# Hash attention and a squared-ReLU MLP: the first pair of heads loaded six tokens to a partition, its successor's preparation and the weight sums placed elsewhere

## The chip, the core and the metric

The kernel runs on one core of a Trainium2 chip. A core has four compute engines that each work through their own instruction stream in order: TensorE (PE, with a separate row PEld for its weight loads), VectorE (DVE), ScalarE (ACT) and GpSimd (POOL). SyncE (SP) issues DMAs, and ACT and POOL issue some too. The metric is device time in microseconds. Before the change it is 879.85 us, the median of three runs (879.66 to 879.92).

## The reference

```python
batch, n_heads, seq, head_dim = (4, 8, 768, 64)       # q, k, v in float32, proj is 64 x 6
n_tokens, d_model, d_ff = (3072, 512, 2048)           # w_in, w_out

q_bits = (np.einsum('bhsd,dk->bhsk', q, proj) > 0)    # k_bits likewise
mask = q_bucket[:, :, :, None] == k_bucket[:, :, None, :]
scores = scale * np.matmul(q, k.transpose(0, 1, 3, 2))
scores = np.where(mask, scores, -1000000000.0)
attn = np.exp(scores - max); attn = attn / (sum + 1e-09)
attn_out = np.matmul(attn, v)
x = attn_out.transpose(0, 2, 1, 3).reshape(B * S, H * D)
h = x @ w_in;  r = np.maximum(h, 0.0);  out = (r * r) @ w_out
```

A query sees only the keys whose six sign bits equal its own. The order of the keys makes no difference to the result, as long as keys and values have the same order.

## The kernel before

**Two stages.** The attention stage (to about 331 us) goes over 16 pairs of heads, `for pr in range(NP)` at L614. The MLP stage after it multiplies by `w_in` and `w_out` with a Strassen-like scheme of seven products in place of eight; its weights' sums are made in the attention stage.

**One pair.** q and k have the two heads' 64 features on 128 partitions and 768 tokens along the row (`feat[pr, 0]` and `feat[pr, 1]`). `hash_bits` (L337) multiplies them by `proj`, `signs` (L351, eight ACT instructions for a pair) turns the products into bits, and `weigh` (L379) scales the keys' bits. For each of six key tiles `kt`, `score(pr, kt)` (L386) puts the product of the bits plus the product of the features into PSUM in two pieces (512 and 256 queries), and ACT takes the exponential of each into a ring of four tiles `e` (L413). `add_up` (L419) sums the tiles on DVE into `total`. `attend` (L432) multiplies by the values. `finish(pr)` (L579) runs one pair late: the column sums of `total` (`tot`, L455), their transpose `flip` and reciprocals on DVE, the last two `attend`s and `spread`. `normalize` (L483) writes `x_t`.

**PSUM.** `turn` (L104) hands out three buffers of two banks in rotation, for the score pieces, the hash products, the first pair's transposes and `tot`. An instruction that writes a buffer waits until the buffer's last reader is done.

**Preparation of the next pair.** From pair 1 on, `features(pr + 1, w)` (L330, a 32 x 32 block transpose on DVE) stands at the head of the round, and `prepare()` (L618: hash products and signs of the next pair) is issued inside `finish`. For pair 0 they stand elsewhere: the two `features(1, w)` before `add_up(0, 1)` (L641), and `prepare()` between `score(0, 2)` and `score(0, 3)` (L656).

**The first pair's start.** Its q and k come in with tokens on partitions: `load_first` (L267) issues q's two heads on the SP and the ACT queue, then k's two heads, then `proj`. Each descriptor is 256 bytes, one token of one head. `first_features` (L302) transposes three 128 x 128 blocks (both heads side by side) into PSUM; ACT copies q's (L316), DVE copies k's (L318). While the first load is on its way `keep_busy(8)` (L323) multiplies ones, and `keep_busy(2)` does so between q's and k's transposes. `first_keys` (L361) makes the keys' bits on DVE for this pair. The program's order on PE: eight busy products, six transposes of q, two busy products, three of k, the hash of q, the hash of k's first half, three transposes of k, the two feature products of key tile 0, its two bit products.

**The weights' sums.** Each pair rounds two pieces of the MLP weights on DVE (`round_weight`, `part_weight`; in the middle `place_power` on ACT). The dictionary `sums` (L542 to L547) says how many of the sixteen sums of the `w_in` factors (`sum_in`, L522: one 128 x 512 DVE operation and two DMAs on SP each) a pair makes: from pair 4 on one, two for pairs 6, 9 and 12, and the rest, two, for pair 15. They stand at the head of the round, ahead of `score(pr, 0)` and `finish(pr - 1)` in DVE's order.

Of the kernel before, what the change touches and what calls it, by code (L numbers as in the profile page):

```python
# [8 lines left out]
FP32 = mybir.dt.float32  # L9
# [25 lines left out]
def kernel(  # L35
# [10 lines left out]
    nc = tc.nc  # L46
    PSUM = bass.MemoryType.PSUM

    B, H, S, D = q.shape
# [3 lines left out]
    P = 128  # L53
    SB = S // P
    HS = S // 2
    NFT = DM // P
    NFF = DFF // P
    NP = B * H // 2
# [12 lines left out]
    ident = glob.tile([P, P], FP32, name="ident")  # L71
# [20 lines left out]
    p_qk = first.enter_context(tc.tile_pool(name="p_qk", bufs=2))  # L92
# [11 lines left out]
    def turn(name):  # L104

        return ps_s.tile([P, 2, 512], FP32, name=name, tag="turn")
# [4 lines left out]
    NIN = 2 * NFT  # L111
# [153 lines left out]
    nat, feat, bits = {}, {}, {}  # L265

    def load_first():  # L267

        for src, name in ((q, "q_nat"), (k, "k_nat")):
            t = p_qk.tile([P, SB, 2, D], FP32, name=name)  # L270
            for h, queue in enumerate((nc.sync, nc.scalar)):
                queue.dma_start(
                    out=t[:, :, h], in_=src[0, h].rearrange("(t p) d -> p t d", t=SB)
                )
            nat[0, name] = t
        for h, queue in enumerate((nc.sync, nc.scalar)):
            queue.dma_start(out=projs[h * D:(h + 1) * D, 0:NBITS], in_=proj)
# [15 lines left out]
    def load_values(pr):  # L293
        b, j = divmod(pr, PB)
        t = p_v.tile([P, 2, SB * D], FP32, name="v_nat")
        nc.sync.dma_start(
            out=t.rearrange("p h (t d) -> p (h t) d", d=D),
            in_=v[b, 2 * j:2 * j + 2].rearrange("h (t p) d -> p (h t) d", t=SB),
        )
        nat[pr, "v_nat"] = t  # L300

    def first_features(w, r):  # L302

        if r == 0:
            feat[0, w] = p_f.tile([P, S], FP32, name=f"feat{w}")
        tp = turn("tp")[:, 0]
        for i in range(SB // 2):
            t = r * (SB // 2) + i
            nc.tensor.transpose(  # L309
                out=tp[:, i * P:(i + 1) * P],  # L310
                in_=nat[0, ("q_nat", "k_nat")[w]][:, t].rearrange("p h d -> p (h d)"),
                identity=ident,
            )
        out = feat[0, w][:, r * HS:(r + 1) * HS]
        if w == 0:
            nc.scalar.copy(out=out, in_=tp[:, 0:HS])  # L316
        else:
            nc.vector.tensor_copy(out=out, in_=tp[:, 0:HS])  # L318

    busy = const.tile([P, 512], BF16, name="busy")  # L320
    void = ps_o.tile([P, 1024], FP32, name="xo")
# [8 lines left out]
    def features(pr, w):  # L330

        feat[pr, w] = p_f.tile([P, S], FP32, name=f"feat{w}")
        nc.vector.transpose(out=feat[pr, w], in_=nat[pr, ("q_nat", "k_nat")[w]])
# [52 lines left out]
    def score(pr, kt):  # L386

        e = ring[len(weights) % NRING]
        weights[pr, kt] = e
        key = slice(kt * P, (kt + 1) * P)  # L390
        sts = []

        def products(st, lo, hi, src, first):
            for h in range(2):
                rows = slice(h * D, (h + 1) * D)
                nc.tensor.matmul(  # L396
                    out=st[:, h, 0:hi - lo], lhsT=src[pr, 1][rows, key],
                    rhs=src[pr, 0][rows, lo:hi], start=first, stop=not first,
                )


        if (pr, kt) == (0, 0):
            for lo, hi in CUTS:
                sts.append(turn("st"))
                products(sts[-1], lo, hi, feat, True)
        for i, (lo, hi) in enumerate(CUTS):
            if len(sts) <= i:
                sts.append(turn("st"))
                products(sts[i], lo, hi, bits, True)
                products(sts[i], lo, hi, feat, False)  # L410
            else:
                products(sts[i], lo, hi, bits, False)
            nc.scalar.activation(  # L413
                out=e[:, :, lo:hi], in_=sts[i][:, :, 0:hi - lo], func=ACTF.Exp, scale=scale
            )
# [3 lines left out]
    def add_up(pr, kt):  # L419

        if kt == 1:
            totals[pr] = p_n.tile([P, 2, S], FP32, name="total")
            nc.vector.scalar_tensor_tensor(
                out=totals[pr], in0=weights[pr, 0][:, :, 0:S], scalar=SB * TINY,
                in1=weights[pr, 1][:, :, 0:S], op0=ALU.add, op1=ALU.add,
            )
        else:
            nc.vector.tensor_tensor(  # L428
                out=totals[pr], in0=totals[pr], in1=weights[pr, kt][:, :, 0:S], op=ALU.add
            )  # L430
# [17 lines left out]
    def sum_up(pr, tot):  # L448


        tot = tot[:, 0]
        for c in range(2):
            for h in range(2):
                g = 2 * h + c
                nc.tensor.matmul(  # L455
                    out=tot[g * 32:(g + 1) * 32, 0:HS], lhsT=ones,
                    rhs=totals[pr][:, h, c * HS:(c + 1) * HS], start=True, stop=True,
                )
        flip = p_n.tile([P, HS], FP32, name="flip")
        nc.vector.transpose(out=flip, in_=tot[:, 0:HS])  # L460
        once = p_n.tile([P, NB], FP32, name="once")
        nc.vector.reciprocal(
            out=once, in_=flip.rearrange("p (n f) -> p n f", f=32)[:, :, 0]
        )
        both = p_n.tile([P, 2, NB], FP32, name="both")
        nc.vector.tensor_tensor(
            out=both, in0=which,
            in1=once.rearrange("p (o n) -> p o n", o=1).to_broadcast([P, 2, NB]), op=ALU.mult,
        )
        onces[pr] = both  # L470
# [72 lines left out]
    todo = list(range(16))  # L543
    sums = {}
    for pr in range(NIN // 2, NP):
        n = 16 if pr == NP - 1 else 1 + (pr % 3 == 0)
        sums[pr], todo = todo[:n], todo[n:]  # L547

    xs = {}
# [22 lines left out]
    def sum_x(i, n):  # L572

        x, (t1, t2, t3) = xs[i]
        lo, hi = slice(0, NCH // 2), slice(NCH // 2, NCH)
        b11, b12, b21, b22 = x[:, 0:2, lo], x[:, 0:2, hi], x[:, 2:4, lo], x[:, 2:4, hi]
        minus(*((t1, b12, b11), (t2, b22, t1), (t3, b22, b12), (b12, b21, t2))[n - 1])

    def finish(pr, beside=None):  # L579

        tot = turn("tot")
        if beside:
            beside()
        sum_up(pr, tot)
        if pr == NP - 1:
            sum_x(0, 2)
            sum_x(0, 3)
        for kt in (SB - 2, SB - 1):
            attend(pr, kt)
        spread(pr)  # L590

    with tc.manual_schedule():
# [21 lines left out]
        for pr in range(NP):  # L614
            a, b = 2 * pr, 2 * pr + 1
            more = pr + 1 < NP

            def prepare():  # L618

                hash_bits(pr + 1, turn("hash"))  # L620
                for w in (1, 0):
                    signs(pr + 1, w)


            if pr + 2 < NP:
                load_pair(pr + 2)
            if pr == X_0:
                load_x(0)
            if more and pr > 0:
                for w in range(2):  # L630
                    features(pr + 1, w)
            if pr > 0:
                round_weight(b - 2)
                load_weight(b)
                for m in sums.get(pr, ()):
                    sum_in(m)
            score(pr, 0)
            if pr == 0:
                first_keys(1, turn("hash"))
            score(pr, 1)  # L640
            if pr == 0:  # L641
                for w in range(2):
                    features(1, w)
            if pr > 0:
                finish(pr - 1, prepare if more else None)
            add_up(pr, 1)
            if pr > 0:
                normalize(pr - 1)


            if pr == X_0 + 1:
                for n in range(2):
                    load_unit(n)
            part_weight(a)
            score(pr, 2)
            if pr == 0:  # L656
                prepare()
            score(pr, 3)
            if more and pr > 0:
                weigh(pr + 1)  # L660
            place_power(a)
            attend(pr, 0)
            attend(pr, 1)
            for kt in (2, 3):
                add_up(pr, kt)
            if more:
                load_values(pr + 1)


            round_weight(a)  # L670
            part_weight(b)
            if more:
                load_weight(a + 2)
            score(pr, 4)
            score(pr, 5)
            if pr == 0:
                weigh(1)
            place_power(b)
            attend(pr, 2)
            attend(pr, 3)  # L680
            add_up(pr, 4)
            add_up(pr, 5)
# [529 lines left out]
        for i in range(NCHUNK):  # L1212
            for s in range(NR):
                r = order(i * NR + s)
# [269 lines left out]
```

## Time and profile before

| what | value |
| --- | --- |
| median of the runs | 879.85 us |
| the profiled execution's own time | 879.66 us |
| its span in the trace | 877.9 us |
| PE busy | 864.8 us of the span |
| DVE busy | 760.4 us |
| ACT busy | 391.5 us |
| mean granted TensorE clock | 0.996 |
| first transposes of q on PE | 4.89 us |
| first exponential on ACT | 11.14 us |
| column sums of pairs 0, 1, 2 (`tot`) | 33.37, 53.28, 73.19 us |
| column sums of pairs 14, 15 | 311.26, 327.52 us |

The profile is of one execution. A row of the timeline has its start and its length in microseconds, the engine (with a q behind the name: the engine's sequencer, which waits or issues DMAs), the source line, the operation, the tiles it writes and reads, the shape, the number of merged instructions, and in brackets the idle time of the engine before it with what ended that. PE's records overlap, since matmuls are pipelined.

### The profile page before, as it was taken

How to read it: one execution, taken by the hardware profiler on the slowest of the kernel's cores; microseconds unless marked ns; L12 is line 12 of the kernel's file. 1: busy time of each engine (PE TensorE's matmuls, PEld its weight loads, DVE VectorE, ACT ScalarE, POOL GpSimd, SP SyncE). 2: the span in 40 equal slices, each digit the busy share in tenths (PEclk: the TensorE clock that was granted, in tenths of full speed). 3: DMA queues.
4: the chain of work that ended last, by engine and by line, in shares of the span. 5: the costliest groups of instructions: out<-in, count | busy, mean ns of one | idle time of the engine just before them, and what ended most of it. 6: DMA issues, size and time to landing. Idle time of an engine off the chain costs nothing.

```text
span 877.9 us, 12130 instructions
## 1 busy us (share of the span) xinstructions
PE 864.8 (99%) x4340; PEld 518.7 (59%) x4340; DVE 760.4 (87%) x1099; ACT 391.5 (45%) x673; POOL 107.0 (12%) x172
## 2 busy tenths in 40 slices
PE   8999999999999999999999999999999999999996
PEld 3444444444444444444688865556888755568885
DVE  5999999999999998888779968888889788888875
ACT  6988888888888852222211123332111233321110
POOL 2000000000000001554231011111000211110002
PEclk9999999999999999999999999999999999999998
DMA  9777967998788536999897764536756754355565
GB/s 176 142 149 134 233 153 156 188 253 225 179 176 225 156 105 213 299 267 283 292 353 239 181 160 168 173 118 222 285 151 187 167 165 155 124 167 154 158 175 105
DMA packets 224131, 167.09 MB, mean 190 GB/s; under 512 B 164448, under 2 KB 181344, under 8 KB 224064
## 3 DMA queue, kind: packets, MB, share of 16 engines
q1 hardware_dynamic: 189152, 87.19, 41.0%
q0 software_dynamic: 12528, 41.30, 15.2%
q10 hardware_dynamic: 22384, 37.76, 14.0%
q8 instruction: 36, 0.59, 0.3%
q14 instruction: 31, 0.25, 0.1%
HBM read 124.52 MB, written 41.68 MB: 189 GB/s over the span
## 4 chain that ended last, share of the span: by engine, by line
PE 95%; DVE 2%; ACT 1%; DMA 1%; issue 0%; ACTq 0%; DVEq 0%
PE acc L712 40%; PE st L396 17%; PE acc L931 16%; PE xo L438 14%; PE acc L884 6%; PE hash L346 2%; PE tot L455 1%; DVE total L428 1%; DMA k_nat<-in_k_dram 1%; ACT bits L356 1%; ACT e L413 0%; PE xo L477 0%; DVE x_t L493 0%; PE tp L309 0%; DVE recs L487 0%
## 5 line engine op out<-in xcount | busy, mean ns | idle before, releaser
L413 ACT ACTIVATE e<-st 128x1024 f32<-128x1024 f32 x192 | 145.1, 810 | 44.9 <-PE st L396 41.0
L396 PE MATMUL st<-feat,feat 64*128 64x512 f32 (+1 forms) x768 | 150.4, 483 | 0.0
L438 PE MATMUL xo<-e,v_nat 128*64 128x512 f32 (+1 forms) x768 | 134.8, 492 | 0.0
L712 PE MATMUL acc<-b,leaf 128*128 128x256 f32 x600 | 133.2, 379 | 0.7 <-issue 0.7
L712 PEld LDWEIGHTS acc<-b,leaf 128*128 128x128 f32 x600 | 113.8, 190 | 17.1 <-issue 1.7
L428 DVE TENSOR_TENSOR total<-total,e 128x1536 f32<-128x1536 f32 x64 | 112.4, 1757 | 8.2 <-ACT e L413 3.6
L438 PEld LDWEIGHTS xo<-e,v_nat 128*64 128x64 f32 x768 | 51.3, 136 | 82.2 <-issue 74.3
L931 PE MATMUL acc<-t_x,w_unit 128*128 128x512 f32 x192 | 90.2, 592 | 0.0
L396 PEld LDWEIGHTS st<-feat,feat 64*128 64x128 f32 x768 | 66.0, 188 | 33.0 <-issue 23.2
L712 PE MATMUL acc<-t,leaf 128*128 128x256 f32 x336 | 76.3, 380 | 0.0
L356 ACT ACTIVATE bits<-hash,lifts 32x384 bf16<-32x384 f32 x120 | 68.6, 572 | 2.3 <-PE hash L346 0.5
L712 PEld LDWEIGHTS acc<-t,leaf 128*128 128x128 f32 x336 | 63.6, 190 | 9.4 <-DVE t L516 0.5
L796 DVE SCALAR_TENSOR_TENSOR b<-h 128x512 f32<-128x512 f32 x96 | 65.7, 691 | 3.0
L396 PE MATMUL st<-bits,bits 64*128 64x256 bf16 (+1 forms) x384 | 63.1, 325 | 1.7 <-ACT e L413 1.2
L931 PE MATMUL acc<-x,w_unit 128*128 128x512 f32 x128 | 60.1, 592 | 0.0
L712 PE MATMUL acc<-x,w_unit 128*128 128x512 f32 x128 | 56.6, 594 | 0.0
L712 PE MATMUL acc<-b_t,leaf 128*128 128x256 f32 x240 | 53.8, 379 | 0.0
L931 PEld LDWEIGHTS acc<-t_x,w_unit 128*128 128x128 f32 x192 | 36.5, 190 | 28.9 <-issue 26.8
L719 ACT COPY two<-acc 128x256 f32<-128x256 f32 (+1 forms) x29 | 12.5, 431 | 87.9 <-PE acc L712 63.1
L719 ACT COPY one<-acc 128x256 f32<-128x256 f32 (+1 forms) x29 | 12.5, 431 | 85.1 <-PE acc L712 46.9
L712 PEld LDWEIGHTS acc<-b_t,leaf 128*128 128x128 f32 x240 | 45.5, 190 | 6.2
L396 PEld LDWEIGHTS <-bits 64*128 64x128 bf16 x384 | 23.5, 93 | 42.5 <-issue 38.4
(159 smaller groups left out, 1165.5 us busy)
## 6 DMA issues: line engine op xcount, KB each, us to landing
leaf<-w_out ACTq DMA_DIRECT2D x142, 256.0 KB, 3.1
w_unit<-w_in SPq DMA_DIRECT2D x16, 640.0 KB, 4.0
raw<-in_moe_w_in_dram SPq DMA_DIRECT2D x16, 512.0 KB, 5.6
raw<-in_moe_w_out_dram SPq DMA_DIRECT2D x16, 512.0 KB, 4.6
w_unit<-w_in SPq DMA_DIRECT2D x8, 896.0 KB, 8.1
w_out<-sums POOLq DMA_DIRECT2D x16, 448.0 KB, 6.8
sum<-w_in SPq DMA_DIRECT2D x16, 448.0 KB, 4.8
v_nat<-in_v_dram SPq DMA_DIRECT2D x16, 384.0 KB, 4.3
```

Source lines behind the costliest of these rows:

```text
L346: nc.tensor.matmul(out=banks[g * NR_B:(g + 1) * NR_B, h, 0:HS], lhsT=projs[rows], rhs=feat[pr, w][rows, c * HS:(c + 1) * HS], start=True, ...
L356: nc.scalar.activation(out=t[h * D:h * D + NR_B, c * HS:(c + 1) * HS], in_=hashed[pr, w][at, h, 0:HS], func=ACTF.Sign, scale=HUGE, bias=li ...
L396: nc.tensor.matmul(out=st[:, h, 0:hi - lo], lhsT=src[pr, 1][rows, key], rhs=src[pr, 0][rows, lo:hi], start=first, stop=not first,)
L413: nc.scalar.activation(out=e[:, :, lo:hi], in_=sts[i][:, :, 0:hi - lo], func=ACTF.Exp, scale=scale)
L428: nc.vector.tensor_tensor(out=totals[pr], in0=totals[pr], in1=weights[pr, kt][:, :, 0:S], op=ALU.add)
L438: nc.tensor.matmul(out=xo[h * D:(h + 1) * D, lo:hi], lhsT=nat[pr, "v_nat"][:, h, kt * D:(kt + 1) * D], rhs=weights[pr, kt][:, h, lo:hi], s ...
L455: nc.tensor.matmul(out=tot[g * 32:(g + 1) * 32, 0:HS], lhsT=ones, rhs=totals[pr][:, h, c * HS:(c + 1) * HS], start=True, stop=True,)
L712: nc.tensor.matmul(out=acc[to], lhsT=a(i), rhs=b(i), start=first and i == 0, stop=last and i == n - 1, skip_group_check=True,)
L719: nc.scalar.copy(out=t, in_=acc[of])
L796: nc.vector.scalar_tensor_tensor(out=out, in0=h, scalar=0.0, in1=h, op0=ALU.max, op1=ALU.mult)
L884: nc.tensor.matmul(out=out, lhsT=w[:, a], rhs=b, start=start, stop=stop, skip_group_check=True)
L931: nc.tensor.matmul(out=acc[to], lhsT=w[:, PLACE[a], f], rhs=bt[b](f), start=first and f == 0, stop=last and f == NFT // 2 - 1, skip_group_ ...
```

## The change

1. The first pair's q, k and v are loaded as `(p t) d`: partition p holds tokens 6p to 6p + 5, in one piece of 1536 bytes a head, in place of six pieces of 256 bytes.
2. The twelve 128 x 128 transposes of the first pair become 24 products of one head's 64 columns with the identity: each writes 64 partitions of PSUM, 128 wide. They are ordinary float32 matmuls, not transposes.
3. ACT's copies of q's features write every sixth column, which brings the queries back into their order. The keys stay in the new order, 128 t + p for token 6p + t, and so do the values.
4. In pair 0, `add_up(0, 1)` comes ahead of `features(1, 0)` and `features(1, 1)` on DVE. For later pairs the order of calls is the same as before.
5. In pair 0, `prepare()` comes behind `score(0, 3)` in place of between `score(0, 2)` and `score(0, 3)`.
6. `sums`: two sums for pair 9 alone (`NIN` is 8), one for each other pair from 4 to 14, and what is left, four, for pair 15.

```diff
@@ load_first
         for src, name in ((q, "q_nat"), (k, "k_nat")):
-            t = p_qk.tile([P, SB, 2, D], FP32, name=name)
+            t = p_qk.tile([P, 2, SB, D], FP32, name=name)
             for h, queue in enumerate((nc.sync, nc.scalar)):
                 queue.dma_start(
-                    out=t[:, :, h], in_=src[0, h].rearrange("(t p) d -> p t d", t=SB)
+                    out=t[:, h], in_=src[0, h].rearrange("(p t) d -> p t d", t=SB)
                 )
@@ load_values
-        nc.sync.dma_start(
-            out=t.rearrange("p h (t d) -> p (h t) d", d=D),
-            in_=v[b, 2 * j:2 * j + 2].rearrange("h (t p) d -> p (h t) d", t=SB),
-        )
+        if pr == 0:
+            nc.sync.dma_start(out=t, in_=v[0, 0:2].rearrange("h (p t) d -> p h (t d)", t=SB))
+        else:
...
@@ first_features
         for i in range(SB // 2):
             t = r * (SB // 2) + i
-            nc.tensor.transpose(
-                out=tp[:, i * P:(i + 1) * P],
-                in_=nat[0, ("q_nat", "k_nat")[w]][:, t].rearrange("p h d -> p (h d)"),
-                identity=ident,
-            )
-        out = feat[0, w][:, r * HS:(r + 1) * HS]
+            for h in range(2):
+                nc.tensor.matmul(
+                    out=tp[h * D:(h + 1) * D, i * P:(i + 1) * P],
+                    lhsT=nat[0, ("q_nat", "k_nat")[w]][:, h, t], rhs=ident, start=True, stop=True,
+                )
         if w == 0:
-            nc.scalar.copy(out=out, in_=tp[:, 0:HS])
+            nc.scalar.copy(
+                out=feat[0, w].rearrange("f (p t) -> f t p", t=SB)[:, r * (SB // 2):(r + 1) * (SB // 2)],
+                in_=tp[:, 0:HS].rearrange("f (t p) -> f t p", p=P),
+            )
         else:
-            nc.vector.tensor_copy(out=out, in_=tp[:, 0:HS])
+            nc.vector.tensor_copy(out=feat[0, w][:, r * HS:(r + 1) * HS], in_=tp[:, 0:HS])
@@ sums
-        n = 16 if pr == NP - 1 else 1 + (pr % 3 == 0)
+        n = 16 if pr == NP - 1 else 1 + (pr == NIN + 1)
@@ the loop over pairs
             score(pr, 1)
+            if pr > 0:
+                finish(pr - 1, prepare if more else None)
+            add_up(pr, 1)
             if pr == 0:
                 for w in range(2):
                     features(1, w)
-            if pr > 0:
-                finish(pr - 1, prepare if more else None)
-            add_up(pr, 1)
...
             score(pr, 2)
+            score(pr, 3)
             if pr == 0:
                 prepare()
-            score(pr, 3)
-            if more and pr > 0:
+            elif more:
                 weigh(pr + 1)
```

More of the change, by code (lines that the diff above doesn't have):

```diff
@@ L295, in load_values @@
         t = p_v.tile([P, 2, SB * D], FP32, name="v_nat")
-        nc.sync.dma_start(
-            out=t.rearrange("p h (t d) -> p (h t) d", d=D),
-            in_=v[b, 2 * j:2 * j + 2].rearrange("h (t p) d -> p (h t) d", t=SB),
-        )
+        if pr == 0:
+            nc.sync.dma_start(out=t, in_=v[0, 0:2].rearrange("h (p t) d -> p h (t d)", t=SB))
+        else:
+            nc.sync.dma_start(
+                out=t.rearrange("p h (t d) -> p (h t) d", d=D),
+                in_=v[b, 2 * j:2 * j + 2].rearrange("h (t p) d -> p (h t) d", t=SB),
+            )
         nat[pr, "v_nat"] = t
@@ L308, in first_features @@
             t = r * (SB // 2) + i
-            nc.tensor.transpose(
-                out=tp[:, i * P:(i + 1) * P],
-                in_=nat[0, ("q_nat", "k_nat")[w]][:, t].rearrange("p h d -> p (h d)"),
-                identity=ident,
-            )
-        out = feat[0, w][:, r * HS:(r + 1) * HS]
-        if w == 0:
-            nc.scalar.copy(out=out, in_=tp[:, 0:HS])
+            for h in range(2):
[3 more added lines that the diff above has]
+                )
+        if w == 0:
+            nc.scalar.copy(
+                out=feat[0, w].rearrange("f (p t) -> f t p", t=SB)[:, r * (SB // 2):(r + 1) * (SB // 2)],
+                in_=tp[:, 0:HS].rearrange("f (t p) -> f t p", p=P),
+            )
         else:
-            nc.vector.tensor_copy(out=out, in_=tp[:, 0:HS])
+            nc.vector.tensor_copy(out=feat[0, w][:, r * HS:(r + 1) * HS], in_=tp[:, 0:HS])
     busy = const.tile([P, 512], BF16, name="busy")
```

## The prediction

> **What bounds the kernel now.** I read the busy shares and the chain of work that ended last first.
>
> ```profile
> PE 864.8 (99%) x4340; PEld 518.7 (59%) x4340; DVE 760.4 (87%) x1099; ACT 391.5 (45%) x673; POOL 107.0 (12%) x172
> ...
> PE 95%; DVE 2%; ACT 1%; DMA 1%; issue 0%; ACTq 0%; DVEq 0%
> ```
>
> PE is the bound. Whatever delays PE in the first pair delays the end by as much, unless PE waits for something else later that takes the delay up. The view of waits, PE alone, lists all such places:
>
> ```profile
> engine line waited for: us in total, times, longest us
> ...
> PE st L396 <- ACT e L413: 1.2, 2, 1.0
> ...
> PE tp L309 <- DMA k_nat<-in_k_dram: 0.5, 1, 0.5
> PE st L396 <- ACT bits L356: 0.5, 1, 0.5
> PE tot L455 <- DVE total L428: 0.4, 1, 0.4
> ```
>
> The first three lie in pair 0, the last in pair 15. Between 33 and 327 us there is no such row: column sums of neighbouring pairs are 19.91 us apart throughout. So the question is pair 0 and pair 15. Pair 0 in the timeline:
>
> ```profile
> 4.89 0.84 PE L309 MATMUL tp<-ident,q_nat 128*128 128x128 f32 x6
> 6.70 0.55 PE L309 MATMUL tp<-ident,k_nat 128*128 128x128 f32 x3 [0.54 <-DMA k_nat<-in_k_dram]
> 8.33 2.35 ACT L356 ACTIVATE bits<-xo,lifts 32x384 bf16<-32x384 f32 x4 [2.03 <-issue]
> 11.14 1.51 ACT L413 ACTIVATE e<-st 128x1024 f32<-128x1024 f32 x2 [0.46 <-PE st L396]
> 14.38 0.94 DVE L333 STREAM_TRANSPOSE feat<-k_nat 128x768 f32<-128x768 f32 x1
> 15.24 1.72 DVE L423 SCALAR_TENSOR_TENSOR total<-e,e 128x1536 f32<-128x1536 f32 x1
> 16.66 4.66 ACT L356 ACTIVATE bits<-hash,lifts 32x384 bf16<-32x384 f32 x8
> 24.17 2.90 ACT L413 ACTIVATE e<-st 128x1024 f32<-128x1024 f32 x4
> 24.57 0.69 DVE L171 SCALAR_TENSOR_TENSOR power<-raw,power 128x512 uint32<-128x512 uint32 x1
> 25.23 0.29 PE L396 MATMUL st<-bits,bits 64*128 64x256 bf16 x2 [0.99 <-ACT e L413]
> 32.59 0.16 PEld L346 LDWEIGHTS hash<-feat,projs 64*32 64x32 f32 x8 [0.47 <-DVE feat L333]
> ```
>
> From 13.50 to 27 us ACT has no idle time: exponentials of tiles 1 and 2, eight signs, those of tile 3, two weight steps (`small`, `power`), those of tiles 4 and 5. PE waits for it. At 32.59 the chain has passed to DVE, whose features of pair 2 end late because `round_weight` (24.57) came late. Pair 15:
>
> ```profile
> 311.13 0.68 DVE L516 TENSOR_TENSOR s_in<-in,s_in 128x512 f32<-128x512 f32 x1
> 312.18 0.58 DVE L460 STREAM_TRANSPOSE flip<-tot 128x384 f32<-128x384 f32 x1 [0.36 <-PE tot L455]
> 317.71 3.62 DVE L428 TENSOR_TENSOR total<-total,e 128x1536 f32<-128x1536 f32 x2
> 327.52 0.85 PE L455 MATMUL tot<-total,ones 128*32 128x384 f32 x8 [0.43 <-DVE total L428]
> ```
>
> DVE runs without a pause from 312.18 to the end of the last `total`, and PE waits for that.
>
> **Term 1, loads and transposes.** *Loads.* Now k lands 5.37 us after its issue at 1.29 (the chain's first piece), and PE stands still 0.54 us for it. The 3072 packets of 256 bytes for q and k take 18 ns each: 3072 x 18 / 16 engines = 3.5 us. There will be 512 of 1536 bytes; packets of 1024 and 2048 bytes take 46 and 84 ns here, so about 65: 2.1 us. k then lands about 1.4 us sooner, near 5.3, and q near 4. Neither shortens the start by itself: q's transposes start at 4.89 because the eight busy products end there (each 0.43 us from 1.48 on), and that stays.
> *Transposes.* Six now start within 0.57 us (0.84 less the last one's 0.27): 0.109 each. No row shows a 128-column product by 64 columns. Nearest is `attend` (L438): also two heads on two halves of the columns, float32, each product in two passes (768 records for 384 products). The two heads' records start 7 ns apart, so they run side by side; 512 moving columns take 0.43 us a pass, 257 take 0.216, so 128 take 0.108, and a block of both heads two passes, 0.216. Lower bound: 0.109, as now. Upper bound: heads one after the other, 0.43. I take 0.216, by the row with the same layout. q: 6 x 0.107 = 0.65 later; the two busy products then end at 6.65, and k's first three start there, not at 6.70: the wait on the DMA is gone, but not the time. These three take 0.32 longer, so k's copy, hash, and with it the signs of q come 0.24 later than now (signs 8.33 to 8.57, ending 10.92). The other three of k stand ahead of tile 0's feature products on PE: 9.15 becomes 9.15 + 0.24 + 0.32 = 9.71. From there to the bit products it is 1.43 now, about 1.4 then: 11.11, behind the signs (10.92), which had been the last to arrive. First exponential: 11.14 becomes about 11.52. **Term 1: +0.38 us.** From both sides: with 0.109 a block, k starts at 6.02, -0.68; with 0.43, q +1.9 and k +1.0 each, less 0.7 of waits, about +2.5.
> *ACT's copies of q* (0.48 each) write every sixth column. No row has such a write; at the same speed they end at 6.90, half a microsecond before hash q needs them at 7.43, and nothing changes. At half speed the second ends at 7.7: +0.25. I take the same speed (nearest row: the copy itself).
> [...]
> v and `proj` land sooner as well: v is first used at 18.09 and has landed by 13.8, so that is worth nothing.
>
> **Term 2, the order in pair 0.** The exponentials of tile 1 end at 15.01 now, 15.40 then (term 1). DVE: `add_up(0, 1)` 15.43, next instruction 1.64 later (as from 15.24 to 16.88 now), the two transposes, 0.90 + 0.94: features done at 18.90, not 15.32. PE and ACT meanwhile do tile 3; ACT is through with it at about 18.7. The hash of k follows the features by 0.06, the first sign 0.92 later (in pair 1: 32.59 to 33.51): 19.88. So ACT stands idle some 1.2 us, where before it had the signs to do. Signs 4.66: to 24.54; `small` and `power`: the first exponential of tile 4 starts 1.31 after the signs' end, at 25.85 in place of 24.17, +1.68. Queued behind the late hash on PE: attends 0 and 1 (needed by nobody soon) and tiles 4 and 5; tile 5's second piece waits for tile 4's buffer as now: 25.23 + 1.68. `power` ends at 25.95, DVE's `round_weight` follows at 25.97, against 24.57: +1.40. It is not +1.68 because DVE was then still adding tile 3, which now is done early. Features of pair 2, hash of k at 32.59: + 1.40, and PE, though 1.68 late, stood waiting there and gets the 0.28 back. **Terms 1 and 2: +1.40 at pair 1's column sums, so term 2 alone is +1.02.** The cover that `features` loses is ACT's own work on tile 2. Ends: if term 1 is 0.25 either way, the sum moves with it; if the signs could start as ACT comes free (18.7), term 2 falls to nothing, if ACT idles 0.3 more, 1.3.
>
> **Term 3, the sums.** Pairs 6, 9 and 12 had two sums; their `flip` came 1.38 behind `tot` in place of 0.92, and PE took no harm: moving those is worth nothing. Pair 15 gets two more. A sum is 0.69, the next starts 0.60 behind it (310.53, 311.13), one that reads its predecessor 0.69: 2 x 0.60 to 0.69 = 1.29 more before `flip`. DVE could have taken `flip` at 311.13 + 0.60 = 311.73 and took it at 312.18, a slack of 0.45, which leaves 0.84; the chain to the last `total` has at most another 0.11 in it (at 317.71 it may be waiting for the exponential). PE's wait at 327.52 grows from 0.43 to about 1.2. **Term 3: +0.80** (0.7 to 0.95). The four extra DMAs on SP are hidden: their factors are read by loads after 331 us, and x_all of pair 14 behind them in SP's queue only in the third chunk. The MLP follows the last `finish` and shifts with it.
>
> **Sum.** 0.38 + 1.02 + 0.80 = +2.2 us on the profiled execution's 879.66 (span 877.9 and 1.8 around it): 881.9. The median of the runs is 0.19 above that execution, so against the median +2.2 would read 882.05; I name 881.9.
>
> **Rivals.**
> A. *The transposes cost no more than now* and the early k pays: -0.68 in place of +0.38, total -0.68 + 1.02 + 0.80 = +1.1: 880.8. For it: pairs of heads side by side, PE's two passes half hidden in its start-up latency. Against: every float32 product of this trace runs in two passes; the transposes of before do not.
> B. *The delays of terms 2 and 3 fall into slack*: ACT fills the gap or DVE catches up; +0.4: 880.0. Against: ACT's row without idle from 13.50, DVE's from 312.18.
> C. *Faster.* Tile 3's exponentials no longer queue behind eight signs (16.66 to 21.32), so PSUM buffers come free 3 us sooner and PE's waits in pair 0 close: 0.54 + 0.24 + 0.48 + 0.99 = 2.25; without term 3: 877.4. It decides only if tile 4's exponentials don't stand behind the signs; on ACT they do, in order.
> D. *Heads one after the other on PE*, or their weight loads in the open: +2.5 in place of 0.38, total +4.3: 884.0. Against: the 7 ns between the heads' records at L438.
>
> **Chances.** Forecast 0.67 (its own range 881.2 to 882.8), A 0.13, B 0.08, C 0.05, D 0.07. Range to 8 in 10: it leaves out B, C and D: 880.6 to 883.4, which holds A. A measurement of this kernel can tell about 0.2%, 1.76 us, from no change. Slower by more: most of the forecast (0.58) and D, 0.65. Same: A, B and the forecast's lower end, 0.30. Faster: C, 0.05.
>
> **What would show it.** Term 1: 0.216 a block, no DMA wait ahead of k, first exponential near 11.5. Term 2: ACT idle over 1 us ahead of pair 1's signs, which start near 19.9, and pair 0's `tot` at 34.8 in place of 33.37. Term 3: four sums, `flip` 0.84 later against `tot`, PE's wait ahead of the last `tot` about 1.2 us. An early first exponential (below 11) or `tot` of pair 0 below 34 would make the prediction wrong.

## The result

The changed kernel takes 883.47 us (median of six runs, 882.32 to 885.39) against 879.7 for the kernel before (879.43 to 879.92): ratio 1.0044, 95% interval 1.0031 to 1.0057, 3.8 us slower. The forecast was 881.9, with a range to 883.4. Its sign was right and its size was not.

The profiled execution took 883.37 us with a span of 881.6. The view of waits, PE alone, answers to the one shown before the prediction:

```profile
engine line waited for: us in total, times, longest us
PE acc L718 <- issue: 1.8, 1, 1.8
...
PE st L402 <- ACT e L419: 1.5, 2, 1.2
PE tot L461 <- DVE total L434: 1.1, 1, 1.1
...
PE hash L352 <- ACT e L419: 0.6, 1, 0.6
PE st L402 <- ACT bits L362: 0.4, 1, 0.4
```

The wait on k's DMA is no longer in PE's list, the one ahead of pair 15's column sums has grown from 0.4 to 1.1, a new one of 0.6 stands ahead of the hash, and the longest of all, 1.8, belongs to the MLP stage. The same view of the kernel before has it with 0.7:

```profile
PE acc L712 <- issue: 0.7, 1, 0.7
```

The timeline of pair 0 in the changed kernel (start, length, engine, line; lines are six later than before):

```profile
4.90 1.53 PE L314 MATMUL tp<-ident,q_nat 128*64 128x128 f32 x24
5.82 1.52 ACT L319 COPY feat<-tp 128x384 f32<-128x384 f32 x2 [2.25 <-PE tp L314]
6.90 1.24 PE L314 MATMUL tp<-ident,k_nat 128*64 128x128 f32 x12
12.21 1.51 ACT L419 ACTIVATE e<-st 128x1024 f32<-128x1024 f32 x2 [0.81 <-PE st L402]
16.11 1.76 DVE L429 SCALAR_TENSOR_TENSOR total<-e,e 128x1536 f32<-128x1536 f32 x1 [1.50 <-ACT e L419]
18.69 0.94 DVE L339 STREAM_TRANSPOSE feat<-k_nat 128x768 f32<-128x768 f32 x1
18.91 1.62 PE L352 MATMUL hash<-feat,projs 64*32 64x384 f32 x16 [0.60 <-ACT e L419]
20.64 4.66 ACT L362 ACTIVATE bits<-hash,lifts 32x384 bf16<-32x384 f32 x8 [1.32 <-issue]
27.82 0.28 PE L402 MATMUL st<-bits,bits 64*128 64x256 bf16 x2 [1.21 <-ACT e L419]
```

The first three blocks of k (six products, each in two records) take 1.24 us here, against 0.88 in the profiles further below. PEld, the row of the weight loads, still waits for k's DMA in the middle of them:

```profile
7.27 0.63 PEld L314 LDWEIGHTS tp<-ident,k_nat 128*64 128x64 f32 x10 [0.18 <-DMA k_nat<-in_k_dram]
```

The first exponential starts at 12.21 (11.14 before), pair 0's column sums at 35.55 (33.37). From the one to the other it is 23.34 us, 22.23 before. So the two profiled executions differ by 12.21 - 11.14 = 1.07 at the start, 23.34 - 22.23 = 1.11 in pair 0, 1.05 - 0.43 = 0.62 in pair 15, and 1.81 - 0.72 = 1.09 in the MLP stage. That is 3.89; the spans differ by 3.7, and the rest of the MLP stage is 0.2 shorter.

Pair 15, DVE's timeline and then PE's, has the four sums in a row and PE's longer wait:

```profile
312.72 0.68 DVE L539 TENSOR_TENSOR s_in<-in 128x512 f32<-128x512 f32 x1
313.44 0.69 DVE L522 TENSOR_TENSOR s_in<-s_in,in 128x512 f32<-128x512 f32 x1
314.05 0.69 DVE L522 TENSOR_TENSOR s_in<-in 128x512 f32<-128x512 f32 x1
314.65 0.68 DVE L522 TENSOR_TENSOR s_in<-in,s_in 128x512 f32<-128x512 f32 x1
315.25 0.58 DVE L466 STREAM_TRANSPOSE flip<-tot 128x384 f32<-128x384 f32 x1
...
317.89 0.98 DVE L493 STREAM_TRANSPOSE recs<-xo 128x768 f32<-128x768 f32 x1
```

```profile
330.33 0.85 PE L461 MATMUL tot<-total,ones 128*32 128x384 f32 x8 [1.05 <-DVE total L434]
```

### The profile page after: what moved, and what is told of

Its sections match the earlier page's. It is cut to its first block, busy times and chain, and to the rows that moved or that the text cites. A ratio compares the mean times of both kernels' runs of the same rounds, so it can differ in the third digit from the quotient of the medians.

```text
span 881.6 us, 12203 instructions
## 1 busy us (share of the span) xinstructions
PE 866.6 (98%) x4376; PEld 520.3 (59%) x4376; DVE 760.6 (86%) x1099; ACT 392.3 (45%) x673; POOL 106.9 (12%) x172
## 4 chain that ended last, share of the span: by engine, by line
PE 95%; DVE 2%; ACT 1%; issue 1%; DVEq 0%
PE acc L718 40%; PE st L402 17%; PE acc L937 16%; PE xo L444 13%; PE acc L890 5%; PE hash L352 1%; PE tot L461 1%; DVE total L434 1%; ACT e L419 1%; ACT bits L362 1%; PE xo L332 0%; PE tp L314 0%; DVE s_in L522 0%; DVE out_piece L179 0%; DVE power L171 0%
```

## The experiments

**Each part alone, and the changed kernel again.** Three kernels take one part each on top of the kernel before: the loads, products and copies (`loads_only`), pair 0's order (`order_only`), the sums (`sums_only`). The diffs here and below show the edits in short.

```diff
 loads_only: load_first, load_values and first_features as changed; order and sums as before
 order_only:
-            if pr == 0: features(1, 0); features(1, 1)
             ... add_up(pr, 1)
+            if pr == 0: features(1, 0); features(1, 1)
             score(pr, 2)
-            if pr == 0: prepare()
             score(pr, 3)
+            if pr == 0: prepare()
 sums_only:
-        n = 16 if pr == NP - 1 else 1 + (pr % 3 == 0)
+        n = 16 if pr == NP - 1 else 1 + (pr == NIN + 1)
```

> The kernel before with the new loads, transposes and strided copies alone. Theory (four causes that add up, each tied to its own part, and the MLP stage's longer wait tied to none of them): first exponential near 12.2 us if k's last two DMA engines are late again (k complete near 7.2), 11.5 if they are not; pair 0's column sums 0.4 to 1.1 us later than 33.37; PE's wait ahead of pair 15's column sums 0.43 as before; total 880.1 to 880.9 with an MLP wait of 0.7. Rival (the MLP wait of 1.8 belongs to the new loads): 1.1 us more, 881.2 to 882.

> The kernel before with the new order of pair 0 alone. Theory: first exponential at 11.14 as before, column sums of pair 0 at 34.4 to 34.5 (+1.1), PE's wait ahead of pair 15's column sums 0.43, MLP wait 0.7; total 880.8. Rival (any displacement of the stage moves the DMAs in the MLP stage against each other, so the MLP wait grows in every variant): MLP wait near 1.8, total near 881.9.

> The kernel before with the new places of the weights' sums alone. Theory: pair 0 as before, PE's wait ahead of pair 15's column sums 1.05 to 1.25 in place of 0.43, MLP wait 0.7; total 880.3 to 880.5. Rival (the four late sums and their eight DMAs cause the longer MLP wait): MLP wait near 1.8, total near 881.5.

> The changed kernel again, with a second profile. Theory: first exponential between 11.5 and 12.3, according to when k's last DMA engines finish; order and sums as in the first profile; MLP wait anywhere from 0.7 to 2, since it hangs on four DMA engines that happened to be late. Rival (all of it fixed by the program): first exponential 12.2 and MLP wait 1.8 again, total 883.4.

| kernel | median us | ratio to before, 95% | first exp. | from it to pair 0's sums | wait, pair 15 | waits, MLP stage |
| --- | --- | --- | --- | --- | --- | --- |
| before | 880.01 | | 11.14 | 22.23 | 0.43 | 0.72 |
| loads_only | 881.18 | 1.0003 to 1.0021 | 13.07 | 22.24 | 0.43 | 0.80 and 0.12 |
| order_only | 881.34 | 1.0003 to 1.0021 | 11.28 | 23.37 | 0.43 | 0.18 and 0.95 |
| sums_only | 880.58 | 0.9994 to 1.0012 | 11.34 | 22.24 | 1.03 | 0.73 and 0.33 |
| after_again | 883.59 | 1.0021 to 1.0044 | 12.99 | 23.37 | 1.03 | 1.10 |

The four right columns are from one execution each (of the kernel before, the first profile). Apart from up to 0.2 at the first exponential and from the MLP stage, each part shows in its own column and in no other: the order adds 1.13, the sums 0.60 (their median alone is not told from none), the loads 1.9 here and 1.07 in the changed kernel's first profile. The medians add up to 1.17 + 1.33 + 0.57 = 3.1 of the 3.6 between the changed kernel and the kernel before in this set. `order_only` came 0.5 us above the 880.8 expected. The wait in the MLP stage goes with no part: from 0.7 to 1.1 in all five here, 1.8 in the first profile. So the rivals that gave a wait of 1.8 to the loads, to the sums or to any displacement fall; the measure of this wait further below says so more firmly.

What I had not expected is the loads' first exponential of 13.07 with k complete at 5.2, and 12.99 in the changed kernel's second profile, where 11.5 to 12.3 was expected. PE's timeline of `after_again` shows why:

```profile
5.00 2.57 PE L314 MATMUL tp<-ident,q_nat 128*64 128x128 f32 x24
7.51 0.60 PE L332 MATMUL xo<-busy 128*128 128x512 bf16 x2
8.04 0.88 PE L314 MATMUL tp<-ident,k_nat 128*64 128x128 f32 x12
```

The same twelve products of q (24 records) that took 1.53 in the first profile take 2.57 here, before the clock is up. Single records start 0.213 apart up to 6.98 and 0.109 apart from 7.19 on; the trace's first clock record, 1.0, begins at 7.17. In the first profile they are 0.109 apart from 5.06 on, and that record begins at 4.73.

**Where the start's time goes.** To part the loads from the products, `products_only` keeps the old loads, order of tokens and plain copies, and has only the 24 products. `loads_no_busy` is `loads_only` without the two busy products between q and k.

```diff
 products_only (on the kernel before), first_features:
-            nc.tensor.transpose(out=tp[:, i * P:(i + 1) * P], in_=...[:, t].rearrange("p h d -> p (h d)"), identity=ident)
+            for h in range(2):
+                nc.tensor.matmul(out=tp[h * D:(h + 1) * D, i * P:(i + 1) * P], lhsT=...[:, t, h], rhs=ident, ...)
 loads_no_busy (on loads_only):
         first_features(0, 1)
-        keep_busy(2)
         first_features(1, 0)
```

> The kernel before with 24 products by the identity in place of 12 transposes, on the old loads and the old token order (no strided copies). Theory (the start is as slow as PE's passes are, and their pace hangs on when the granted clock reaches 1.0): two passes a block, 0.109 each after that moment and 0.213 before it; first exponential 11.5 to 11.7 where the clock is up by 5 us, 12.9 to 13.1 where it comes near 7.2; total 880.2 to 881.6. Rival (k's late landing or the strided copies made the start slow): first exponential 11.1 to 11.3 whatever the clock, total 879.8.

> The new loads and products on the old order and sums, without the two busy products between q and k. Theory (PE's own work is the chain of the start, k is there by 5.3): k's products follow q's at once, first exponential 0.4 to 0.6 sooner than with them at the same clock: 11.6 to 11.8 with an early clock, 12.4 to 12.6 with one near 7.2; total 880.0 to 880.7. Rival (the DMA of k is the chain): PE waits for k in their place, first exponential 12.2 to 13.1 as before.

`products_only`: 881.13 (1.0006 to 1.0024), first exponential 12.83. `loads_no_busy`: 880.74 (1.0003 to 1.0021), first exponential 11.28. PE's timeline of `products_only`, then of `loads_no_busy`:

```profile
5.01 2.41 PE L310 MATMUL tp<-ident,q_nat 128*64 128x128 f32 x24
7.35 0.61 PE L326 MATMUL xo<-busy 128*128 128x512 bf16 x2
7.88 0.88 PE L310 MATMUL tp<-ident,k_nat 128*64 128x128 f32 x12
```

```profile
4.99 1.53 PE L314 MATMUL tp<-ident,q_nat 128*64 128x128 f32 x24
6.36 0.82 PE L314 MATMUL tp<-ident,k_nat 128*64 128x128 f32 x12
7.50 0.53 PE L352 MATMUL xo<-feat,projs 64*32 64x384 f32 x4 [0.32 <-ACT feat L319]
```

The products alone cost 1.26 in the median, as much as the whole of `loads_only` (1.17): the new descriptors bring nothing back, because k is not what PE waits for. The start of `loads_no_busy` is earlier than the 11.6 to 11.8 expected, since the two busy products cost more than their own 0.43: from q's last product to k's first it is 0.74 us with them (7.30 to 8.04 in `after_again`) and 0.11 without (6.25 to 6.36). All starts side by side, with the moment of the first clock record:

| execution | loads | records of q | clock record from | k complete | q on PE, first to last start | k on PE | first exp. |
| --- | --- | --- | --- | --- | --- | --- | --- |
| before | old | 6 | 4.56 | 6.66 | 4.89 to 5.46 | 6.70 | 11.14 |
| order_only | old | 6 | 7.03 | 6.73 | 4.87 to 5.94 | 7.00 | 11.28 |
| sums_only | old | 6 | 6.48 | 6.98 | 4.87 to 5.94 | 7.02 | 11.34 |
| products_only | old | 24 | 6.85 | 6.47 | 5.01 to 7.14 | 7.88 | 12.83 |
| changed, first | new | 24 | 4.73 | 7.23 | 4.90 to 6.16 | 6.90 | 12.21 |
| after_again | new | 24 | 7.17 | 5.27 | 5.00 to 7.30 | 8.04 | 12.99 |
| loads_only | new | 24 | 7.34 | 5.20 | 5.01 to 7.38 | 8.12 | 13.07 |
| loads_no_busy | new | 24 | 4.92 | 5.69 | 4.99 to 6.25 | 6.36 | 11.28 |
| after_x_later | new | 24 | 5.94 | 5.29 | 5.01 to 6.70 | 7.44 | 12.39 |
| prepare_late | old | 6 | 4.53 | 6.59 | 4.71 to 5.25 | 6.63 | 11.10 |
| features_late | old | 6 | 4.42 | 6.85 | 4.65 to 5.20 | 6.89 | 11.21 |
| before_x_later | old | 6 | 6.58 | 6.49 | 4.87 to 5.94 | 6.80 | 11.06 |
| before_x_prep | old | 6 | 4.19 | 6.68 | 4.78 to 5.36 | 6.72 | 11.18 |

With the old transposes a late clock costs at most 0.2 us (rows 2 and 3; none in `before_x_later`), since it only fills the time that PE waits for k anyway. With 24 products there is nothing to wait for: k's first product comes up to 1.22 later with a late clock (8.12 against 6.90). In the four profiles with 24 products, the two busy products and k complete ahead of its first product, the first exponential follows that product by 4.95; in the changed kernel's first profile it is 5.31. So 0.36 of that profile's start is k's late load, and the clock's price is 1.2, not the 0.9 between the first exponentials (13.07 and 12.21). Without the busy products and with an early clock the start is nearly as early as before, and now ACT's strided copies (0.85 and 0.88) are what PE waits for, 0.32.

The table has the same two paces as `after_again`, 0.213 ahead of the clock record and 0.109 behind it: q's six old records take 1.07 from first to last start where that record begins at 6.48 or later, and 0.54 to 0.58 where it begins by 4.56. It has no fixed place. In the thirteen executions profiled here, all with busy products from 1.48 on, it begins anywhere from 4.19 to 7.34, a spread of 3.15 us, from 2.71 to 5.86 behind the first busy product.

**The order, halved.** `prepare_late` has only the hash products and signs behind tile 3, `features_late` only the features behind `add_up(0, 1)`.

```diff
 prepare_late (on the kernel before):
             score(pr, 2)
-            if pr == 0: prepare()
             score(pr, 3)
+            if pr == 0: prepare()
 features_late (on the kernel before):
-            if pr == 0: features(1, 0); features(1, 1)
             ... add_up(pr, 1)
+            if pr == 0: features(1, 0); features(1, 1)
```

> The kernel before with the next pair's hash products and signs behind tile 3, its features where they were. Theory (what the new order costs is ACT standing idle until DVE's late features, not the signs' place): with the features early the signs follow tile 3's exponentials at once, ACT has no gap over 0.3 us, the first exponential of tile 4 starts where it did, pair 0's column sums within 0.3 us of before once the start of the clock is taken off (first exponential to column sums 22.2 us), total 880.0. Rival (signs behind tile 3 cost by themselves, since PE's hash and attends move back): first exponential to column sums 23.0 or more, total 881.

> The kernel before with the next pair's features behind add_up(0, 1), its hash products where they were, ahead of tile 3. Theory: PE now waits in front of tile 3 for the features (near 18.9), tile 3's exponentials stand behind the signs, so nothing covers the gap: ACT idle about 3 us, first exponential to column sums 24.5 to 25.5, total 882 to 883. Rival (the features are a small cost wherever they stand): first exponential to column sums under 23.5.

`prepare_late`: 879.66 against 879.8 (ratio 0.9989 to 1.0007), first exponential to column sums 22.07. `features_late`: 883.29 (1.0022 to 1.0049), 25.81, somewhat more than expected. ACT's timeline of `prepare_late`, then of `features_late`:

```profile
13.47 4.75 ACT L413 ACTIVATE e<-st 128x1024 f32<-128x1024 f32 x6 [0.85 <-PE st L396]
18.25 4.67 ACT L356 ACTIVATE bits<-hash,lifts 32x384 bf16<-32x384 f32 x8
```

```profile
20.30 4.66 ACT L356 ACTIVATE bits<-hash,lifts 32x384 bf16<-32x384 f32 x8 [3.60 <-issue]
```

Signs behind tile 3 cost nothing as long as DVE has the features ready: ACT goes from the sixth exponential to the signs without a gap. Late features cost ACT 3.60 of idle time if `prepare` stays early, and 1.32 if it moves too. Part of the 3.60 is the clock. `features_late` is the only one of the thirteen profiles with a clock record of 0.5 ahead of the kernel's end, from 18.07 to 21.49, right behind the 2.22 us for which PE waits there. Its hash products, then those of `order_only`, in PE's timelines:

```profile
17.91 2.27 PE L346 MATMUL hash<-feat,projs 64*32 64x384 f32 x16 [2.22 <-DVE feat L333]
```

```profile
17.99 1.62 PE L346 MATMUL hash<-feat,projs 64*32 64x384 f32 x16 [0.60 <-ACT e L413]
```

From the first hash product to the first sign it is 2.39 against 1.73 us. Without these 0.66 ACT's gap would be 2.9 and the stretch to the column sums 25.15, both as expected (an estimate from these rows). Whether the pause of PE brings the record about was not tried, nor whether the other executions of `features_late` have it. So the late `prepare` takes back 2.45 of the 3.58 that late features cost in this profile (25.81 to 23.36), some 0.66 of which goes with the record of 0.5.

**The wait in the MLP stage.** DVE's timeline of the changed kernel shows what is late: the sums of two factors of `w_in` (L516, `factor_units`) wait for their loads, and the additions that free PE's accumulators stand behind them in order. POOL's timeline shows these loads issued right behind the second chunk's x, 2 MB.

```profile
448.49 1.22 DVE L522 TENSOR_TENSOR b_t<-b_t 128x1024 f32<-128x1024 f32 x1
452.06 0.42 DVE L516 TENSOR_TENSOR h<-h 128x256 f32<-128x256 f32 x1 [2.35 <-DMA h<-w_in]
...
454.67 0.42 DVE L1014 TENSOR_TENSOR tmp<-acc,one 128x256 f32<-128x256 f32 x1
```

```profile
437.05 0.95 POOL L560 DMA_DIRECT2D x<-x_all  x1
437.81 1.28 POOL L843 DMA_DIRECT2D h<-w_in  x2
```

The slower of the two loads takes 13.7 us in the changed kernel and 12.6 in the kernel before; the next two of the same kind, with no x ahead of them, take 3.8 to 5.6 (a later one 8.1 in the kernel before). x itself lands after 12.9 and 11.9. `before_x_later` and `after_x_later` load x for the second chunk three products later and sum it one product later.

```diff
-                if k == 0 and i + 1 < NCHUNK:
+                if k == (3 if i == 0 else 0) and i + 1 < NCHUNK:
                     load_x(i + 1)
-                if k in (3, 4) and i + 1 < NCHUNK:
-                    sum_x(i + 1, 2 * k - 5); sum_x(i + 1, 2 * k - 4)
+                kk = k - (1 if i == 0 else 0)
+                if kk in (3, 4) and i + 1 < NCHUNK:
+                    sum_x(i + 1, 2 * kk - 5); sum_x(i + 1, 2 * kk - 4)
```

> The kernel before with the second chunk's x loaded three products later, behind the loads of the first-level factors, and its sums one product later. Theory (DVE stands in order behind the sums of two factors whose loads share the DMA engines with x's 2 MB, and PE waits for DVE; how long differs by execution, 0.7 to 1.8): the wait near 451 us goes, total 879.2 to 879.4 with a smaller spread. Rival (the wait is the leaf's own load, or the DMAs just wait elsewhere): a wait of 0.5 us or more stays in that stage, total as before, 880.0.

> The changed kernel with the same later load of x. Theory: the wait near 454 us (1.8 and 1.1 in its two profiles) goes, total 1.1 to 1.8 less than the changed kernel, 882 to 882.4. Rival as for the kernel before: no gain.

The kernel before: 878.44 (878.04 to 879.02 over eleven runs, against 879.1 to 880.72; ratio 0.9974 to 0.9992). The changed one: 881.91. In both profiles the wait is gone and none takes its place; the two loads now take 5.7 to 6.1 us. PE's timeline of `before_x_later` in that stretch, then the kernel before's row that answers to the last one:

```profile
443.08 3.62 PE L712 MATMUL acc<-t,leaf 128*128 128x256 f32 x16
446.54 5.34 PE L712 MATMUL acc<-b,leaf 128*128 128x256 f32 x24
451.71 3.62 PE L712 MATMUL acc<-b_t,leaf 128*128 128x256 f32 x16
```

```profile
452.71 3.62 PE L712 MATMUL acc<-b_t,leaf 128*128 128x256 f32 x16
```

This gained more than the 0.6 to 0.8 expected: 1.36 in the median. The view of waits shows less than the wait costs. From pair 15's column sums to the first `acc<-b_t` product it is 124.24 or 124.25 us in the three profiles with the later load, and 125.06 to 126.33 in the ten others: 0.8 to 2.1 more, 1.3 on average, 0.95 in the kernel before and 2.09 in the changed kernel's first profile. It doesn't go with a displacement of the stage: `prepare_late`, whose stage starts 0.2 sooner than the kernel before's, has 1.48, and `sums_only`, 0.8 later, has 0.97. The wait's size differs from execution to execution. The kernel before spreads over 1.6 us in this set, and over 1.0 with the later load, so the wait may be part of that spread.

With the wait out of both, the change still costs 881.91 - 878.44 = 3.5 us. In the median the wait thus had only a few tenths of the changed kernel's 3.8. The two profiles without it differ by 3.3 in their spans: 1.33 at the first exponential, 1.09 from there to pair 0's column sums, 0.61 in pair 15, and some 0.3 behind.

**Both edits that did not lose.**

> The kernel before with the later load of x and with prepare behind tile 3, features early: the two edits that did not lose, together. Theory: no wait near 451 us (-1.4, as measured alone) and first exponential to column sums 22.07 (-0.17): total 878.2 to 878.4. Rival (prepare's place is worth nothing, its 0.17 was the noise of one execution): 878.4 to 878.6, not to be told from the later load alone.

`before_x_prep` takes 878.47 (878.06 to 878.75; ratio 0.9975 to 0.9993). That is `before_x_later` again: the place of `prepare` can't be told from nothing, and the rival holds. Both take 1.4 us less than the kernel before of their sets.

## Why the prediction was right or wrong

- **What bounds it: right in pair 0 and pair 15, incomplete behind.** That PE's delays go through to the end holds: pair 0's and pair 14's column sums are 277.89 us apart in both kernels (the step is 19.91 thirteen times and 19.10 the last time, not 19.91 throughout). But the prediction said that its view listed all places where PE waits, and passed over the row of 0.7 us at L712 in it. "The MLP follows the last `finish` and shifts with it" is the step that failed there: the wait stands behind two 256 KB loads of which the slower takes 12.6 us next to x's 2 MB in the kernel before and 13.7 in the changed one, and such a wait doesn't simply shift. It was 1.09 longer in the changed kernel's first profile and 0.38 longer in its second, but only a few tenths by the medians.
- **Term 1, loads and transposes: wrong in size, 0.38 forecast, 1.07 to 1.9 measured in profiles and 1.17 in the median.** The arithmetic of 0.216 a block is right where the clock is up (0.218 measured), side by side for the two heads. What failed is the step that took PE's clock at 4.89 from one execution: "that stays" was said of the busy products' end, and the pace after it was taken as the fast one. In eight of thirteen profiles the clock record begins after 4.89, in seven of them at 5.9 us or later. Before that moment a block costs 0.427. Even with the clock up the sum was short. In the changed kernel's first profile k's first product starts at 6.90 and not at 6.65: q's products take 0.14 longer than worked out and the two busy products 0.53 in place of 0.43. From there to the first exponential it is 4.95, not 4.87, where k is in time. That makes 11.85, an estimate from these rows: +0.71 in place of +0.38. The other 0.36 of the 1.07 is k's load. It behaved as worked out in four of five profiles (k complete at 5.2 to 5.7, forecast 5.3), but in this one fourteen of the sixteen reports of the head that lands last had come by 5.46 and the last two at 6.60 and 7.23. Two packets took 845 and 974 ns there (the median is 65), but the last packet of 1536 bytes ended at 5.57, so they alone don't explain it, and the cause stays open. That no time is won by an earlier k, as the prediction had it, was right. Terms 2 and 3 are off by about +0.1 and -0.2, so nearly all that the forecast misses lies in this term and in the MLP stage.
- **ACT's copies:** the forecast took the same speed and named half speed as the other end. Measured 0.84 to 0.88 against 0.48, so the other end was the nearer one. With the same products but plain copies, `products_only` has 0.48, so the time goes with the new way of writing; by what in it, no run shows. As forecast, it doesn't delay the changed kernel: the second copy ends at 7.34, the hash starts at 8.07.
- **Term 2, the order: right.** +1.02 forecast, +1.11 to 1.14 measured, ACT idle 1.32 (1.2 forecast). The cause was shown by the halves: it is the features, not the place of `prepare`.
- **Term 3, the sums: right in kind, 0.80 forecast, 0.60 to 0.62 measured.** `flip` came 0.88 later in `sums_only`, as worked out. On the way to the last `total` there was more slack than the 0.11 counted: at `recs`, which had waited for PE's `spread`, 0.15 went as well.
- **Rivals:** A (transposes cost no more) falls: `products_only` shows their price. B falls: no part was hidden. C falls: `prepare_late` shows that tile 3 ahead of the signs wins at most 0.17. D, heads one after the other, falls by the records, 7 ns apart; but its price, a block at 0.43, is what a late clock makes of it.

## What to carry to other kernels

Work at this kernel's very start ran at either of two paces, records 0.213 or 0.109 us apart, as the clock record came anywhere from 4.19 to 7.34, and one profile shows one draw: price such work at both paces, and ask which wait covers the slow one. PE's wait in the MLP stage, which hangs on a DMA, had no fixed length: 0.72 us in the kernel before's profile, 1.81 in the changed kernel's first. Where such a DMA is issued behind a large one, as here behind 2 MB, look at who is queued in order behind the waiting engine, and try the large one later (the kernel before gained 1.36 us by it in the median). Ahead of moving a producer, see which engine's own work covered it: the signs could move for nothing (22.07 us from the first exponential to the column sums, 22.23 before), the features could not (25.81).

## What the runs showed of the hardware that I had not expected

The first clock record of 1.0 begins between 4.19 and 7.34 us with busy products from 1.48 on in all thirteen profiles. In one of them a record of 0.5 lasts 3.42 us in pair 0, and the sixteen records of hash products there take 2.27 us in place of 1.62. In five profiles the 512 packets of 1536 bytes for q and k took 65 ns in the median and 72 to 77 on average, but single ones 845 and 974, and k was complete only with the last of sixteen reports. ACT copies 128 x 384 from PSUM in 0.48 us to a row without gaps and in 0.84 to 0.88 to every sixth column. Two 256 KB loads issued 0.8 and 1.3 us behind a 2 MB load took 11.9 to 13.7 us in ten profiles; with the 2 MB load moved away they took 5.3 to 6.1.
